# Fp16 queries from PSUM for the first two groups, short zero products in PSUM slots of their own, and a new issue order

## The chip, the cores and the metric

The kernel runs on one core of a Trainium2 chip. The metric is the device time of one execution in microseconds (us): the median of several runs. The engines of the core are named as the profile names them: PE (matrix products and transposes, with PEld for its weight loads), DVE, ACT and POOL (elementwise work), and SP, whose queue (SPq in the profile) issues all DMAs of this kernel. Each engine executes its own instructions in the order in which they stand in its queue. An instruction that waits for a semaphore holds up everything behind it on its engine.

## The reference

Two stages are chained. The first is an attention with chunk selection over q, k, v of shape (4, 8, 768, 64): batch, head, token, dimension. Keys are cut into 24 chunks of 32. For each chunk the smallest and the largest key per dimension give an upper bound on the score:

```python
ub = np.sum(np.maximum(q[..., None, :] * k_min, q[..., None, :] * k_max), axis=-1)
ub = np.where(causal, ub, -1000000000.0)
top_chunks = np.argsort(ub, axis=-1)[..., -6:]
scores = scale * np.matmul(q, k.transpose(0, 1, 3, 2))
scores = np.where(sel & (pos[:, None] >= pos[None, :]), scores, -1000000000.0)
attn = softmax(scores); attn_out = np.matmul(attn, v)
```

The second takes the attention output as x (4, 768, 512), and mixes tokens and channels:

```python
theta = x @ w_theta
y = einsum('ts,bsd->btd', w_tok_r, x * cos(theta)) + einsum('ts,bsd->btd', w_tok_i, x * sin(theta))
u = x + y
out = u + np.maximum(u @ w_ch, 0.0)
```

## The kernel before, in words

Heads are handled in groups of four: group (b, g) is heads 4g to 4g+3 of batch b, so there are eight groups. A group is prepared by these steps.

- `load_kc` (L276), `load_q` (L285) and `load_v` (L295) fetch keys, queries and values in fp32. One `q32` buffer holds a pair of heads; its two loads are one per head.
- `keys` builds the chunk maxima and minima on DVE (L315, L320, L324), transposes them (L339) into `bnd`, casts the keys to fp16 on POOL (L351) and transposes them on PE (L359); ACT or DVE evicts them to `kext` (L365). Rows 64 to 87 of `kext` are a constant one-hot pattern times -1000, loaded by DMA (L766), which is needed before any scores of that `kext` buffer.
- `queries` transposes the fp32 queries on PE into the PSUM tile `psq` (L394). ACT (L402) or DVE (L404) makes the positive and the negative part in fp32 for the bounds (`ubq`). The fp16 queries for the scores come in one of two ways. For groups in the set `QPE` (before: only (0, 0)), ACT or DVE casts them out of the same `psq` tile straight into `qext` (L410), and block 0, which the bounds do not need, is transposed too. For the others, POOL casts the queries untransposed into `qe` (L381), and a DMA transpose takes them from there to `qext` (L479).
- `choice` makes the bounds (`psub`, L432), adds the causal mask (L440), transposes (L446), finds the sixth largest bound (L454) and marks the chunks below it (L468). For `QPE` groups the marks go to a small tile, are transposed on PE (`pss`, L492) and evicted to rows 64 to 87 of `qext` by ACT or DVE (L497, one instruction per head). For the others they are written into `qe` and travel with the queries in the DMA transpose L479, of which a group has two, one for each pair of heads.

`attend` then works head by head: scores (`psc`, L533) in three PSUM tiles from a pool of two slots ("sc"); exp on ACT (L542); the causal triangle of the diagonal blocks on POOL (L553); the product with the values (`psav`, L564); the division on DVE (L575, L580). When the eight heads of a batch are there, x is transposed (PE L608 or DMA L597) and `phases` computes theta (`pst`, L628), sine and cosine on ACT (L636) and their products with x on DVE (L642). `mixer` does the token product (L670, L672), the channel product (L706) and the output. The token weights are cast on POOL (L731), transposed on PE (L743) and evicted (L747); they share the 'w32' and 'a16' buffers. All short-lived PSUM tiles come from a pool of three slots ("mi").

At the start, `FILL` zero products (L832) of 128x128 by 128x512 keep PE at work while it waits for data. They write one tile of the pool "sc" and read a zeroed tile of the tag "cs".

All of this is registered as tasks with `plan.add`. `Plan.emit` does not sort: the constant tuple `ORDER` lists the task numbers in the order of issue (a negative number sends an eviction that may run on either engine to DVE instead of ACT). The durations, due times and latencies given to `plan.add` have no effect on the program: they served the planner that wrote `ORDER`. Each engine's queue is its part of that list.

Of the kernel before, what the change touches and what calls it, by code (L numbers as in the profile page):

```python
# [9 lines left out]
FP32 = mybir.dt.float32  # L10
FP16 = mybir.dt.float16
ALU = mybir.AluOpType
AF = mybir.ActivationFunctionType
# [62 lines left out]
def kernel(  # L76
# [14 lines left out]
    P = 128  # L91
# [22 lines left out]
    for r in range(96):  # L114
# [40 lines left out]
        18, 0, 14, 17, 16, 2, 19, 8, 1, 7, 9, 54, 3, 20, 4, 21, 5, 22, 83, 55, 23, 6, 15, 84, 188, 117, 24, 72,  # L155
        25, 86, 87, 26, 27, 85, 58, 28, 73, 29, 88, 190, 30, 74, 62, 31, 60, -90, 32, 118, 76, 67, 64, 119, 75,
        65, 66, 63, 61, 56, 90, -72, 91, 77, 96, 69, 33, 93, 57, 34, 78, 35, 70, 36, 120, 37, -100, 68, 38, 189,
        39, 10, 79, 98, 40, 41, 80, 94, 42, 121, 43, -93, 44, 191, 11, 45, -98, 95, 81, 146, 82, 297, 100, 101,
        192, 150, 13, 102, 106, 59, 103, 46, 104, 194, 107, 296, 115, 47, 131, 48, 130, 108, 132, 49, 122, 50,
        133, 105, 154, 109, 137, 110, 298, 51, 111, 151, 52, 53, 138, -115, -114, 174, 124, 193, 147, 175, 180,  # L160
        299, 139, 116, 125, 112, 140, -149, 181, 126, 252, 134, 300, 123, 253, 258, 195, 196, -153, 182, 135,
        177, 127, 259, 141, 178, -150, 176, 266, 129, -154, 260, 136, 128, 142, 155, 310, 200, 254, 255, 156,
        311, 12, -158, 313, 329, 143, 179, -313, 183, 316, 314, 415, 158, 267, -316, 184, 144, 256, 280, 185,
        334, 159, 172, 145, 272, 186, 160, 257, 281, 301, 161, 268, 302, 335, 336, 187, 317, 283, 416, 273, 417,
        284, 269, 318, 304, 325, 261, 337, 197, 262, 418, 339, 286, 166, 162, 204, 270, 319, 167, 163, 419, 338,
        263, 201, 264, 164, 326, 327, 282, 265, 271, 165, 328, 168, 274, 287, 173, 169, 202, 170, 285, 330, 203,
        320, 198, 199, 288, -333, 429, 303, 275, -332, 276, 322, 431, 305, 448, 321, 294, 208, 277, -296, 308,
        -431, 444, 453, 323, -455, 306, 456, 278, 324, 279, 205, 458, 171, 353, -456, 309, 457, 359, 354, 289,
        307, 340, 351, 360, 626, 435, 212, 356, 420, 290, 367, 357, 355, 291, 423, 206, 341, 292, 368, 627, 373,
        209, 361, -208, 374, 370, 293, 345, 216, 436, 371, 381, 625, 342, 358, -383, 383, 343, 369, 389, 384,  # L170
        346, 372, 344, 390, 386, 375, 347, 362, 432, 364, 387, 385, 210, -435, 363, 391, 348, 397, 333, 365, 349,
        639, 398, 366, 213, -212, 376, 378, 641, -434, 377, 352, 403, 628, 379, 214, 404, 421, 400, 217, -216,
        640, 629, 401, 422, 218, 642, -220, 405, 388, 220, 445, 644, 380, 350, 449, 402, 643, 437, 392, 394, 399,
        450, 393, 472, 395, 658, 224, 396, 473, -447, 406, 408, 424, 428, 654, 407, -452, 447, 478, 475, 409,
        410, 474, 411, 476, 413, -413, 663, -415, 479, 666, 477, -665, 486, 667, -666, 470, 668, 582, 487, 490,
        221, 480, 452, 228, 222, 585, 743, 488, 425, 491, 494, 492, 489, 426, -224, 225, 481, 498, 495, 427, 496,
        493, 744, 226, 232, 502, -228, 229, 499, 630, 500, 483, 482, 497, 236, 506, 632, 501, 503, 510, 631, 504,
        484, 471, 485, 511, 507, 745, 230, 505, 508, 512, 634, 438, 583, 522, 523, 524, 509, 525, 233, 513, 514,
        586, 439, 240, 515, 588, 441, 635, 231, 516, 596, 237, 526, 440, 589, 527, 584, 244, 597, 587, 234, 528,
        633, 637, 599, 442, 590, 600, 602, 443, 238, -236, 746, 241, 591, 593, -240, 636, 610, 645, 517, 246,  # L180
        459, 518, 742, 603, 646, 242, 611, 604, 460, 592, 613, 594, 464, 680, 243, 461, 616, 462, 465, 614, 534,
        601, 747, 245, 535, 463, 617, 536, 247, 466, 248, 558, 598, 250, 559, 595, 537, 618, 647, 624, 605, 607,
        612, 538, 467, 539, 615, 540, 249, 606, 560, 546, 468, 608, 651, 609, 547, 251, 561, 748, 548, 648, 619,
        519, 469, 649, 562, 520, 946, 563, 650, 549, 638, 521, 682, 564, 683, 621, 762, 620, 685, 550, 686, 551,
        688, 681, 552, 652, 689, 696, 653, 751, 529, 763, 697, 702, 669, 947, 690, 622, 623, 749, 530, 687, 764,
        754, 703, 699, 684, 756, 670, 700, 750, 711, 698, 674, 759, -758, 671, 704, 712, -759, 714, 672, 662,
        691, 693, 692, 655, 760, 761, 673, 701, 949, 717, 715, 694, 531, -657, 768, 771, 695, 718, 675, 532, 705,
        657, 706, 713, 676, 725, 707, 719, 753, 533, 728, 726, 708, 677, 541, 716, 710, 659, 709, 553, 660, 731,
        -543, 720, 722, 678, 775, 727, 543, 554, -662, 732, 721, 765, 570, 729, 950, 776, 571, 739, 723, 544,
        730, 572, 573, -779, 733, 772, 752, 724, 574, 975, 948, -774, 575, 799, 576, 797, 734, 735, 736, 800,  # L190
        -778, 555, 755, 737, 951, 774, 738, 802, 679, 801, 556, 740, 803, 780, -742, 798, 783, 805, -785, 813,
        804, 806, 545, -786, 955, 1064, 903, 807, -782, 814, -783, 557, 766, 565, 953, 808, 817, -567, 1065, 767,
        815, 917, 818, 821, 816, 819, 825, 820, 822, 823, 966, 829, 826, 827, 567, 824, 833, 828, 830, 831, 568,
        809, 834, 569, 810, 577, 835, 769, -579, 954, 832, 904, 579, 770, 779, 952, 958, 786, 580, 1066, 967,
        918, 787, 906, 791, 788, 907, 837, 789, 792, 909, 790, 910, 931, 838, 793, 848, 911, 932, 839, 811, 968,
        908, 849, 840, 794, 920, 905, 919, 841, 812, 795, 921, 934, 972, 912, 836, 913, 935, 937, 850, 969, 796,
        842, 938, 851, 922, 843, 852, 957, 979, 914, 923, 915, 1067, 960, 916, 924, 976, 844, 853, 961, 925,
        1003, 978, 854, 1006, 1001, 926, 855, 1004, 870, 970, 871, 1007, 872, -963, 581, 927, -978, 1063, 984,
        928, 1009, 1008, 945, -986, 873, 1010, 929, 939, 874, 875, 1011, 956, 1017, 876, 933, 1068, 1020, 1018,
        930, 987, 936, 845, -990, -987, 1005, 1021, -989, 1019, 940, 942, 963, 846, 941, 983, 980, 943, -966,  # L200
        1023, 881, 1022, 1024, 971, 882, 964, 883, 944, 884, -983, 859, 1031, 1002, 885, 981, 1012, 1096, 847,
        860, 886, 887, 1069, 861, 1032, 1083, 1033, 862, 973, 863, 892, 974, 864, 865, 893, 1084, 1038, 866, 894,
        1039, 1035, 1085, 1013, 856, 1036, 1072, 1086, 895, 877, 896, 897, 959, 1014, 857, 867, 898, 1075, 858,
        1089, 888, 1015, 1025, 990, 868, 1092, 1016, 899, 878, 991, 1034, 1040, 995, 992, 879, 1046, 1026, 869,
        993, 1028, 1047, 1077, 1073, 1052, 996, 994, 1074, 1078, 1027, 1053, 1054, 1048, 997, 1049, 880, 889,
        1079, 1050, 998, 1080, 1037, 1029, 890, 999, 900, 1081, 1051, 1030, 1082, 1097, 901, 1093, 1098, 1000,
        1087, 1041, 1101, 1043, 1099, -1095, 1042, 1044, 1060, 1045, 1095, 1104, 1088, 1055, 1057, 1106, 1070,
        1120, 1103, -1106, 1090, 1102, 891, 1056, 1121, 1091, 1126, 902, 1058, 1107, 1059, 1127, 1128, 1061,
        1108, 1123, 1062, 1112, 1122, 1109, 1113, 1124, 1110, 1134, 1111, 1125, 1100, 1230, 1135, 1224, 1114,
        1129, 1130, 1138, 1115, 1136, 1117, 1142, 1139, 1137, 1146, 1140, 1143, 1071, 1141, 1150, 1144, 1147,  # L210
        1145, 1148, 1151, 1154, 1131, 1149, 1158, 1152, 1159, 1155, 1160, 1161, 1156, 1169, 1225, 1170, 1171,
        1132, 1157, 1153, 1172, 1076, 1162, 1173, 1231, 1116, 1163, 1174, 1175, 1227, 1164, 1226, 1202, 1228,
        1133, 1232, 1203, 1165, 1119, 1204, 1238, 1180, 1229, 1176, 1118, 1233, 1239, 1234, 1181, 1205, 1252,
        1191, 1253, 1235, 1192, 1244, 1236, 1254, 1237, 1245, 1241, 1240, 1206, 1242, 1246, 1207, 1243, 1267,
# [12 lines left out]
        1405, 1406, 1417, 1418,  # L227
    )
    PHK = -2
    FILL = 34  # L230

    UDMA = {(b, t) for b in (1, 2) for t in range(NT)} | {(3, t) for t in range(4)}
    XDMA = {(b, c) for b in (1, 2, 3) for c in range(3)}
# [655 lines left out]
```

## Time and profile before

| | us |
|---|---|
| median of 6 runs | 263.17 |
| lowest, highest | 262.22, 265.62 |
| the profiled execution, its own time | 263.93 |
| its span, first to last instruction | 262.2 |
| PE busy | 231.5 |
| DVE, ACT, POOL busy | 179.8, 159.7, 132.8 |

The profile page gives busy times by engine, then the span in 40 slices, the DMA queues, the chain of work that ended last, the costliest groups of instructions by line, and the DMA issues. A line of a group reads: line, engine, operation, output<-input, shapes, count, then busy time and the mean duration of one in ns, then the idle time of the engine just before and what ended it. A line of a timeline reads: start, duration, engine, line, operation, and in square brackets the idle time before it and its releaser. A line of the windows reads: stretch, length, busy time (and instructions) of PE, PEld, DVE, ACT and POOL, the granted PE clock, the busy share of the DMA engines and their GB/s.

### The profile page before, as it was taken

The numbers are of one execution on the slowest core, as the hardware profiler recorded it, in microseconds if no ns is written. First come the engines' busy times: TensorE is split into PE (matmuls) and PEld (weight loads), VectorE is DVE, ScalarE is ACT, GpSimd is POOL, SyncE is SP. The second block draws the span as 40 slices with busy tenths as digits, with TensorE's granted clock in tenths as the row PEclk, the third lists the DMA queues.
The fourth block names the chain that finished last, engine by engine and source line by source line (L and its number), as shares of the span: only waits on it lengthen the run. The fifth ranks groups of instructions, "written<-read, shape, count | busy, mean of one in ns | idle before, by whom it ended". The sixth has DMA issues, their size and how long they took to land.

```text
span 262.2 us, 5663 instructions
## 1 busy us (share of the span) xinstructions
PE 231.5 (88%) x2123; PEld 144.0 (55%) x2123; DVE 179.8 (69%) x470; ACT 159.7 (61%) x225; POOL 132.8 (51%) x188
## 2 busy tenths in 40 slices
PE   3877678688779999999989999997899999999993
PEld 1444365557655566577645666554654666644441
DVE  2779958758654988998997968669673335663362
ACT  2553858639659884299589765417698677654001
POOL 4366568776766658698920767263132554400000
PEclk9999569659979999999999999999999999999999
DMA  6998989999997999995974397477733206730234
GB/s 177 247 227 193 212 194 244 210 182 225 211 210 204 256 220 247 177 230 130 199 201 114 62 199 174 104 119 184 191 71 65 43 0 113 180 123 0 78 82 160
DMA packets 96674, 42.32 MB, mean 161 GB/s; under 512 B 89848, under 2 KB 90104, under 8 KB 95976
## 3 DMA queue, kind: packets, MB, share of 16 engines
q1 hardware_dynamic: 96648, 41.98, 72.9%
q8 instruction: 16, 0.26, 0.5%
q14 instruction: 10, 0.08, 0.1%
HBM read 26.30 MB, written 6.29 MB: 124 GB/s over the span
## 4 chain that ended last, share of the span: by engine, by line
PE 61%; DMA 15%; DVE 7%; ACT 7%; POOL 4%; SPq 4%; issue 2%; DVEq 0%; POOLq 0%; ACTq 0%
PE psc L533 11%; PE psy L670 8%; PE psy L672 8%; PE psav L564 6%; PE pst L628 6%; PE pso L706 5%; DMA qext<-qe 5%; PE psub L432 3%; SPq L295 3%; DMA out_dram<-ot 2%; DMA w<-in_moe_w_tok_i_dram 2%; PE psz L670 2%; PE psz L672 2%; DMA q<-in_q_dram 2%; PE psq L394 2%
## 5 line engine op out<-in xcount | busy, mean ns | idle before, releaser
L542 ACT ACTIVATE pt<-psc 128x1024 f16<-128x1024 f32 (+1 forms) x96 | 85.1, 920 | 45.7 <-PE psc L533 42.8
L553 POOL TENSOR_TENSOR pt<-pt,tri 128x256 f16<-128x256 f16 x96 | 65.4, 699 | 53.9 <-ACT pt L542 53.6
L533 PE MATMUL psc<-qext,kext 88*128 88x512 f16 (+3 forms) x256 | 55.6, 328 | 6.3 <-DMA qext<-qe 3.0
L533 PEld LDWEIGHTS <-kext 88*128 88x128 f16 x256 | 34.5, 154 | 22.2 <-issue 9.6
L670 PE MATMUL psy<-zz,wtokT 128*128 128x512 f16 x120 | 45.5, 379 | 0.0
L672 PE MATMUL psy<-zz,wtokT 128*128 128x512 f16 x120 | 45.4, 378 | 0.0
L564 PEld LDWEIGHTS <-pt 128*128 128x128 f16 x672 | 30.7, 101 | 8.1 <-POOL pt L553 0.9
L564 PE MATMUL psav<-v,pt 128*128 128x65 f16 x672 | 33.2, 198 | 1.0 <-DVE x L580 0.5
L402 ACT ACTIVATE ubq<-psq,signs 128x384 f32<-128x384 f32 (+1 forms) x38 | 18.2, 511 | 14.1 <-PE psq L394 14.0
L642 DVE TENSOR_TENSOR zz<-x,cs 128x1024 f16<-128x1024 f16 x24 | 17.4, 734 | 12.4 <-ACT cs L636 12.3
L706 PE MATMUL pso<-wch,uT 128*128 128x512 f16 x96 | 24.5, 379 | 1.3 <-ACT uT L698 0.5
L628 PE MATMUL pst<-wtheta,xT 128*128 128x512 f16 x96 | 23.3, 378 | 0.8 <-ACT cs L636 0.8
L315 DVE TENSOR_TENSOR h<-kc 96x1024 f32<-96x1024 f32 (+1 forms) x16 | 20.0, 1251 | 4.3 <-DMA kc<-in_k_dram 4.2
L394 PE MATMUL psq<-ident,q 128*128 128x128 f32 x82 | 17.0, 316 | 6.2 <-issue 2.1
L670 PEld LDWEIGHTS <-wtokT 128*128 128x128 f16 x144 | 14.1, 98 | 13.5 <-issue 0.7
L711 DVE SCALAR_TENSOR_TENSOR ot<-pso,u 128x512 f32<-128x512 f32 x24 | 16.5, 687 | 7.4 <-PE pso L706 4.9
L672 PEld LDWEIGHTS <-wtokT 128*128 128x128 f16 x144 | 14.0, 98 | 13.2 <-issue 0.2
L682 DVE TENSOR_TENSOR u<-psy,x 128x512 f16<-128x512 f32 x20 | 13.7, 689 | 10.9 <-PE psy L672 10.9
L636 ACT ACTIVATE cs<-pst,pi 128x512 f16<-128x512 f32 x24 | 16.7, 695 | 7.0 <-PE pst L628 6.1
L351 POOL CAST ke<-kc 96x1024 f16<-96x1024 f32 x16 | 17.2, 1079 | 3.7 <-DMA kc<-in_k_dram 2.7
L506 POOL CAST v<-v 128x768 f16<-128x768 f32 x16 | 15.0, 937 | 7.7 <-DMA v<-in_v_dram 4.4
L575 DVE RECIPROCAL rec<-psav 128x6 f32<-128x6 f32 x32 | 6.1, 191 | 18.4 <-PE psav L564 18.3
(72 smaller groups left out, 341.6 us busy)
## 6 DMA issues: line engine op xcount, KB each, us to landing
v<-in_v_dram SPq DMA_DIRECT2D x64, 96.0 KB, 3.9
q<-in_q_dram SPq DMA_DIRECT2D x32, 192.0 KB, 3.9
out_dram<-ot SPq DMA_DIRECT2D x24, 256.0 KB, 2.3
kc<-in_k_dram SPq DMA_DIRECT2D x7, 768.0 KB, 7.5
w<-in_moe_w_tok_r_dram SPq DMA_DIRECT2D x6, 384.0 KB, 4.3
w<-in_moe_w_tok_i_dram SPq DMA_DIRECT2D x6, 384.0 KB, 5.6
w<-in_moe_w_theta_dram SPq DMA_DIRECT2D x4, 256.0 KB, 6.4
w<-in_moe_w_ch_dram SPq DMA_DIRECT2D x4, 256.0 KB, 4.2
```

Source lines behind the costliest of these rows:

```text
L315: nc.vector.tensor_tensor(out=st[hn].rearrange("p (z w) d -> p z (w d)", z=2)[:, s], in0=kv[:, s, 0], in1=kv[:, s, 1], op=op)
L394: nc.tensor.transpose(t[:, o * P:(o + 1) * P], st[q32][:, n, :, :].rearrange("p x d -> p (x d)"), ident32)
L402: nc.scalar.activation(out=o, in_=i_, func=AF.Relu, bias=0.0, scale=signs[:, y:y + 1])
L533: nc.tensor.matmul(t[:, a0:a1], kx[0:KX, hj:CH * 96:NCH], qx[0:KX, q0 + a0 - o:q0 + a1 - o], start=True, stop=True)
L542: nc.scalar.activation(out=t[:, BASE[s]:BASE[s] + wa + wb], in_=st[psc][:, 0:wa + wb], func=AF.Exp, bias=0.0, scale=scale)
L553: nc.gpsimd.tensor_tensor(out=d, in0=d, in1=tri16.unsqueeze(1).broadcast_to([P, 2, P]), op=ALU.mult)
L564: nc.tensor.matmul(t[:, a, :], st[pt][:, o:o + P], v16s[g][:, x, j, :], start=(j == 0), stop=(j == a))
L628: nc.tensor.matmul(p, st[xT][:, c, t * P:(t + 1) * P], wtheta16[:, c, :], start=(c == 0), stop=(c == 3))
L642: nc.vector.tensor_tensor(out=st[zz][:, t, :, :].rearrange("p i (c d) -> p i c d", d=P), in1=st[cs].rearrange("p i (c d) -> p i c d", d=P) ...
L670: nc.tensor.matmul(acc(), wtokT16[:, i, 0, t * P:(t + 1) * P], st[zz][:, i, 0, :], start=(i == 0), stop=False)
L672: nc.tensor.matmul(acc(), wtokT16[:, i, 1, t * P:(t + 1) * P], st[zz][:, i, 1, :], start=False, stop=(i == NT - 1))
L706: nc.tensor.matmul(p, st[uT][:, c, :], wch16[:, c, :], start=(c == 0), stop=(c == 3))
```

## The change

Three things are edited. `QPE` now holds (0, 1) as well as (0, 0), so that the second group of batch 0 takes the way through PSUM. The zero products get a persistent zeroed tile `zero16`, `FILL` falls from 34 to 24, and six new tasks `rest` of two zero products each (together 36 products) write tiles of the pool "mi". `ORDER` is replaced as a whole; the assignment of evictions to ACT or DVE changes with it (241 tasks on ACT instead of 217, 295 on DVE instead of 307). One latency given to the planner changes, without effect on the instructions.

```diff
     ORDER = (
-        18, 0, 14, 17, 16, 2, 19, 8, 1, 7, 9, 54, 3, 20, 4, 21, 5, 22, 83, 55, 23, 6, 15, 84, 188, 117, 24, 72,
...
+        0, 1, 3, 8, 50, 2, 4, 5, 114, 6, 54, 52, 115, 113, 193, 7, 15, 17, 13, 14, 51, 18, 20, 21, 22, 47, 53,
...
-    FILL = 34
+    FILL, REST = 24, 6
...
-    QPE = {(0, 0)}
+    QPE = {(0, 0), (0, 1)}
...
-            dma(key, 786432 // parts, 280, go, w=[(n, z)], nw=[n] if z == 0 else [], lat=2.8)
+            dma(key, 786432 // parts, 280, go, w=[(n, z)], nw=[n] if z == 0 else [], lat=1.9 if parts == 2 else 2.8)
...
-    fz = ("cs", "zero")
-    plan.add("DVE", 0.45, -9.5, lambda: nc.vector.memset(new(fz), 0.0), w=[(fz, 0)], new=[(fz, "cs")])
-    plan.add("ACT", 1.5, -9.5, lambda: nc.scalar.activation(out=dmy, in_=st[fz][:, 0, 0:1], func=AF.Exp, bias=0.0,
-                                                            scale=1.0), r=[(fz, 0)], w=["table"], kind="exp")
+    zero16 = per.tile([P, dm], FP16, name="zero16", tag="zero16")
+    plan.add("DVE", 0.45, -9.5, lambda: nc.vector.memset(zero16, 0.0), w=["zero"])
+    plan.add("ACT", 1.5, -9.5, lambda: nc.scalar.activation(out=dmy, in_=zero16[:, 0:1], func=AF.Exp, bias=0.0,
+                                                            scale=1.0), r=["zero"], w=["table"], kind="exp")
     for i in range(FILL):
         def fill(i=i):
             t = newp(("fill",), "sc", [P, 1024], FP32) if i == 0 else st[("fill",)]
-            nc.tensor.matmul(t[:, 0:512], st[fz][:, 0, 0:P], st[fz][:, 0, :], start=True, stop=True)
-        plan.add("PE", 0.43 if i < 8 else 0.22, 0, fill, r=[(fz, 0), "ident32"], w=[(("fill",), 0)],
+            nc.tensor.matmul(t[:, 0:512], zero16[:, 0:P], zero16, start=True, stop=True)
+        plan.add("PE", 0.22, -9.4 + 0.2 * i, fill, r=["zero"], w=[(("fill",), 0)],
                  new=[(("fill",), "sc")] if i == 0 else [])
+    for i in range(REST):
+        def rest(i=i):
+            t = newp(("rest", i), "mi", [P, dm], FP32)
+            for _ in range(2):
+                nc.tensor.matmul(t, zero16[:, 0:P], zero16, start=True, stop=True)
+        plan.add("PE", 2 * dm * MM, -3 + i * 0.6, rest, r=["zero"], w=[(("rest", i), 0)], new=[(("rest", i), "mi")])
     prepare(0, 0)
```

What the new order does to the queues up to the first scores of batch 1, read from the lists of both programs. SP: before the second one-hot load (L766) stand 9.52 MB of loads instead of 8.73; up to and with the last query load of batch 1 10.41 MB instead of 11.00; up to and with the first DMA transpose of group (1, 0) 14.53 MB instead of 15.22, of which 0.79 MB are the two transposes that no longer exist. ACT: 31 instructions stand before the first exp instead of 19, among them the casts of all four query pairs of batch 0. PE: the scores of heads 4 to 7 of batch 0 begin right behind the transposes of the second group's marks; the transposes of the last query pair of batch 1 stand behind the first scores of head 4 instead of ahead of them. From the first theta product on, PE's list has the same work.

## The prediction

> **What bounds the kernel now.** I read the stretches first, each engine's busy time between marks that I chose at the first scores, at the two halves of batch 0, and where PE gets dense:
>
> ```profile
> 0.00:25.00 25.00, 16.70 (x119) 9.05 (x120) 16.64 (x47) 10.50 (x20) 13.33 (x28) 1.00 0.97 206
> 25.00:55.00 30.00, 22.21 (x205) 16.69 (x204) 22.91 (x60) 19.53 (x30) 19.73 (x28) 0.71 1.03 215
> 55.00:80.00 25.00, 20.66 (x257) 15.74 (x256) 16.34 (x54) 17.49 (x24) 18.02 (x25) 0.87 1.14 220
> 80.00:135.00 55.00, 52.93 (x548) 34.31 (x547) 47.44 (x122) 40.24 (x55) 40.06 (x52) 1.00 0.89 203
> 135.00:230.00 95.00, 91.23 (x864) 55.63 (x863) 62.53 (x172) 64.12 (x84) 41.69 (x59) 1.00 0.54 118
> ```
>
> From 80 us on PE is busy 96% at full clock: 182 us that only less PE work would shorten. Before 80 us PE has gaps, its clock sags to 0.71, and the one thing that is full is the DMA share, 0.97 to 1.14 at 206 to 220 GB/s. So the start is paced by transfers and what waits for them; a gain there moves the dense part forward whole. Next the chain that ended last, for that part:
>
> ```profile
> 28.77 4.16 SPq L295
> ...
> 48.15 4.88 DMA q<-in_q_dram
> ...
> 53.16 0.66 PE psq L394 x2
> ...
> 66.29 8.28 DMA qext<-qe
> ...
> 74.61 0.60 PE psc L533 x3
> ```
>
> It runs through SP's full queue, the last query load of batch 1 (landing at 53.03), its transposes, and the DMA transpose of group (1, 0), which lands 8.28 us after its issue and starts batch 1's scores at 74.61. The first theta product follows at 79.48. Last, the path that the change removes:
>
> ```profile
> 48.66 3.57 SPq L479 DMA_TRANSPOSE qext<-qe  x1
> ...
> 55.62 2.11 SPq L479 DMA_TRANSPOSE qext<-qe  x1
> ```
> ```profile
> 54.41 0.83 POOL L381 CAST qe<-q 128x768 f16<-128x768 f32 x1 [1.18 <-DMA qext<-qe]
> ```
>
> The marks of group (0, 1) are done on DVE at 47.8, its first transpose lands at about 54.4, and PE starts head 4's scores at 54.58; ACT is idle for 4.03 us before that.
>
> [...] six zero products from 7.03 take 2.56 us, 0.427 each; thirteen from 13.87 take 2.97, 0.228 each. But the granted clock reads 1.00 in both places, so that column is no proof in the first 10 us. [...] here L410 is on ACT and DVE alone. [...] here L479 lands after 3.7 to 8.3, median 4.3. [...]
>
> **The change part by part.** All durations are from the profiled execution (263.93 us, 1.73 more than its span, 0.76 above the median). I form a difference in its span and take it from the median.
>
> *Group (0, 1) through PSUM.* Gone: two POOL casts (L381, mean 868 ns: 1.74 us), two DMA transposes (5.68 us of SP issue, 0.79 MB). New: two fp32 transposes of block 0 (three take 0.49, so 0.33 us) and five fp16 ones (L492, 0.45) on PE; eight casts L410, seven on ACT (0.474) and one on DVE (0.559): 3.88 us; four evictions L497, three on ACT (0.681), one on DVE (0.49): 2.53. ACT gets 5.4 us, DVE 1.1, PE 0.8. In the first 25 us ACT is busy 10.50, and it idles 4.03 before 54.87: cover is there. Not all of it: the casts stand ahead of the first exp and the last ones wait for a load; I put the first exp (25.40) 1 to 2 us later. Without cover the ACT part would cost 5.4. After this delay the (0, 1) scores could start when marks (47.8), transposes and evictions are through: 47.8 less the 2 to 3 us by which its bounds stand nearer the front, plus 0.45 and 0.7, about 46 to 47; the second one-hot load, 0.79 MB later at 215 GB/s, is issued 3.7 us later than 38.26 and lands by about 46 as well. So head 4 starts near 47 instead of 54.58. That is 7.5 us for the half batch, but not for the end.
>
> *What is late next.* The last query load of batch 1 has 0.59 MB less ahead of it: 2.7 us, landing at 50.3. PE's queue has its transposes behind head 4, so PE may wait there for some 2 us at half work, which costs nothing against 54.58. The first transpose of group (1, 0) has 0.69 MB less ahead: 0.69 / 0.22 = 3.1 us, issue at 63.2, landing by the same 8.28 at 71.5 instead of 74.57. The second half's exps and triangles end earlier than that: POOL has 1.74 us less and begins them 5 to 7 us sooner, so the last value product stands behind batch 1's scores, as before. The bounds for the gain at this point are 0 (if q's landing doesn't move) and 5.5 (if the load queue empties and the landing takes the median 4.3). I take 3.1 and add 0.4 for a part of the shorter landing: 3.5.
>
> *Zero products.* 36 instead of 34, 0.216 warm: 0.4 us, while PE is busy only 16.70 of the first 25. I cost it at nothing; uncovered 0.4. The new "mi" tiles have no reader, so their slots are free at the product's end; a wait for a slot costs at most two products, 0.43. Their gain by the clock: the granted clock loses 30 x 0.29 + 25 x 0.13 = 12 us of half speed between 25 and 80; PE was waiting for most of it. I take zero, with bounds of a loss of 0.4 and a gain of 4 (a third).
>
> *The order after 80 us.* Same PE work, 14 further evictions moved from DVE to ACT beyond the ten above, the same eight table loads. Edits in the dense part can only add or remove waits: PE idles 2.1 us in 80 to 135 and 3.8 in 135 to 230, so at most 5.9 can be won, and ACT's load bounds the loss (below). I take zero. At the end, one output now stands ahead of the transpose of u's fourth block on SP; its product starts 0.4 us later than PE could. I charge 0.2 for that, as PE has other products to do there. Sum: -3.5 + 0.2 = -3.3, and 263.17 - 3.3 = **259.9**.
>
> **The rivals.** *The gain is eaten by the loads* (262.5): the stage is paced by bytes, and the transpose of (1, 0) stays tied to marks that come after the bounds of (1, 0), queued on PE behind more second-half scores than before. For it: PE's queue is strict and q lands only 2.7 us earlier. Against: 0.79 MB really leave. Gain 0.7. *The clock comes too* (255): psub took 2.0 us at 56.5 and 1.25 later; if the new order keeps PE warm from 25 to 80, 4 us of queued PE work go as well, 3.5 + 4 + some. Against: PE has idle time there anyway. *ACT becomes the limit* (267, slower): ACT gets 24 more instructions of about 0.6 us, 14 us, on 159.7. Exps stand behind them, only two score slots exist, and PE's strict queue stops when a slot is late. Today PE waits for exp 1.1 us in all. A third of the 14 us exposed costs 4.8; with 0.9 lost from the late first exp and none of the start gained, about 267. It decides from the point where these waits exceed the 3.5 us gained. Against: ACT is busy 40.24 of 55 in the densest stretch.
>
> **How the numbers follow.** Forecast 0.52, loads 0.23, clock 0.10, ACT 0.15. A measurement of this kernel tells about 1% (2.6 us) from no change: faster means below 260.5. The forecast lies there in about 0.8 of its cases (0.42), the clock case always (0.10), the loads case seldom (0.02): 0.54. Within 1%: 0.10 + 0.20 = 0.30. Slower: 0.15 and a remainder of the loads case, 0.16. The range runs from 254.5 (the clock case's centre, the bounds 5.5 plus part of 4) to 265.5 (loads case with a loss), leaving out most of the ACT case and the far side of the clock case. The forecast's own range is 257.7 (the gain of 5.5) to 262.5.
>
> **What would show it.** Right: L479 twelve times, L381 twelve; head 4's scores near 47; the transpose of (1, 0) issued near 63 and batch 1's scores near 71; the first theta product near 76; PE dense from there for the same 182 us. Wrong: head 4 early but batch 1's scores at 74 (loads); granted clock near 1 from 25 on and PE work shorter (clock); waits of L533 for L542 of several us after 80 (ACT). The forecast fails as well if the dense stretch, re-ordered throughout, has other waits than before.

## The result, and the profile after

The changed kernel took 261.81 us in the median of 28 executions (257.54 to 265.34), the kernel before, beside it, 263.93 (63 executions). The ratio of the changed kernel's time to that of the kernel before is 0.9914, 95% interval 0.9883 to 0.9945: 0.9% faster, 2.1 us by the medians, where 3.3 were forecast. Run again later, beside other kernels, it gave 259.74 against 261.60 us, ratio 0.9954 (0.9917 to 0.9991). Both kernels spread over some 8 us from one execution to the next; the ratios leave out executions more than 1.5% above the fastest of their kernel, the medians don't, and where the two disagree both are given.

The profiled execution took 264.52 us (span 262.6), more than the median, and so its time can't be set against before's 263.93. The same stretches as before, each engine's busy time between the marks:

```profile
0.00:25.00 25.00, 17.50 (x121) 8.99 (x122) 17.05 (x49) 14.34 (x30) 12.28 (x26) 1.00 1.01 208
25.00:55.00 30.00, 23.64 (x244) 17.54 (x245) 22.99 (x59) 25.22 (x38) 23.55 (x30) 0.77 1.01 216
55.00:80.00 25.00, 20.80 (x234) 16.48 (x232) 14.00 (x48) 16.38 (x24) 17.14 (x23) 0.73 1.04 217
80.00:135.00 55.00, 52.97 (x535) 33.78 (x534) 47.10 (x117) 42.87 (x60) 35.55 (x50) 1.00 0.95 202
135.00:230.00 95.00, 93.07 (x889) 57.74 (x888) 61.05 (x170) 68.39 (x92) 40.75 (x59) 1.00 0.53 115
```

The DMA share ahead of 80 us is as full as before. ACT has taken on work: 25.22 of the 30 us from 25 to 55, instead of 19.53. The granted clock from 55 to 80 fell from 0.87 to 0.73. Between 135 and 230 PE is busy 93.07 us instead of 91.23.

The chain that ended last, for the part that the forecast spoke of:

```profile
40.83 6.73 DMA kext<-onehot
...
47.61 1.93 PE psc L533 x6
...
62.42 9.60 DMA qext<-qe
72.02 0.04 issue
72.06 1.01 PE psc L533 x3
```

Head 4's scores start at 47.61 (forecast 47, before 54.58), released by the second one-hot load. The transpose of group (1, 0) is issued at 62.42 (forecast 63.2), and batch 1's scores start at 72.06 (forecast 71.5, before 74.61). So far the forecast holds. PE's timeline from there to the first theta product, with idle times in brackets:

```profile
62.24 0.50 PE L743 MATMUL pw<-ident,a 128*128 128x128 f16 x6
64.71 0.66 PE L394 MATMUL psq<-ident,q 128*128 128x128 f32 x2 [1.97 <-DVE x L580]
...
72.06 1.01 PE L533 MATMUL psc<-qext,kext 88*128 88x512 f16 x3 [0.92 <-DMA qext<-qe]
...
79.03 1.02 PE L628 MATMUL pst<-wtheta,xT 128*128 128x512 f16 x4
```

The first theta stands at 79.03, where 76 was forecast: 7 us after batch 1's scores instead of 4.9. In the kernel before it was:

```profile
79.48 1.02 PE L628 MATMUL pst<-wtheta,xT 128*128 128x512 f16 x4
```

So the scores came 2.55 us earlier and the first theta only 0.45. The three products at 72.06 take 1.01 us; at 25.36 three of them took 0.60. The clock explains most of it; the stretches of one microsecond around it, columns as above:

```profile
63.00:64.00 1.00, 0.00 (x0) 0.00 (x0) 1.00 (x3) 0.75 (x1) 1.00 (x3) 1.00 0.79 149
64.00:65.00 1.00, 0.29 (x2) 0.32 (x3) 0.72 (x1) 0.00 (x0) 1.00 (x2) 0.57 1.05 210
...
77.00:78.00 1.00, 1.00 (x8) 0.68 (x6) 0.58 (x2) 0.64 (x1) 0.21 (x1) 0.61 1.17 268
78.00:79.00 1.00, 1.00 (x19) 0.94 (x17) 0.58 (x2) 0.06 (x1) 0.86 (x2) 1.00 1.35 337
```

PE falls to half clock within the gap of 1.97 us in front of 64.71 and stays there for 13.7 us, from 64.1 to 77.8 (worked out from the means of 0.57 and 0.61). Two later profiles, shown below, tell what this cost between batch 1's scores and the first theta. The same list of instructions took 4.66 us at full clock (66.90 to 71.56), instead of 6.97. The list of the kernel before took 4.06 at full clock (71.13 to 75.19) and 4.87 in the first profile, where it too fell to half clock, from 75.1 to 78.5. So of the 2.1 us by which this stretch grew, 0.6 is work that the new order put into it and 1.5 is the clock.

### The profile page after: what moved, and what is told of

The parts are those of the page before. It is cut to its first block, busy times and chain, and to the rows that moved or that the text cites. A ratio compares the mean times of both kernels' runs of the same rounds, so it can differ in the third digit from the quotient of the medians.

```text
span 262.6 us, 5705 instructions
## 1 busy us (share of the span) xinstructions
PE 234.0 (89%) x2132; PEld 145.6 (55%) x2132; DVE 173.9 (66%) x458; ACT 173.0 (66%) x249; POOL 129.3 (49%) x186
## 4 chain that ended last, share of the span: by engine, by line
PE 62%; DMA 12%; ACT 12%; DVE 9%; issue 2%; POOL 1%; SPq 1%; ACTq 0%; DVEq 0%
PE psc L533 13%; PE psy L670 9%; PE psy L672 8%; PE psav L564 6%; PE pso L706 6%; PE pst L628 6%; DMA qext<-qe 4%; ACT pt L542 4%; PE psub L432 3%; DMA uT<-u 3%; ACT ubq L402 3%; DMA kext<-onehot 3%; PE psq L394 2%; ACT cs L636 2%; PE psz L670 2%; DVE h L315 2%
## 5 line engine op out<-in xcount | busy, mean ns | idle before, releaser
L542 ACT ACTIVATE pt<-psc 128x1024 f16<-128x1024 f32 (+1 forms) x96 | 85.0, 918 | 31.9 <-PE psc L533 27.7
L533 PE MATMUL psc<-qext,kext 88*128 88x512 f16 (+3 forms) x256 | 55.3, 336 | 8.7 <-DMA kext<-onehot 3.7
L533 PEld LDWEIGHTS <-kext 88*128 88x128 f16 x256 | 34.9, 153 | 23.9 <-issue 8.0
L706 PE MATMUL pso<-wch,uT 128*128 128x512 f16 x96 | 26.2, 400 | 3.7 <-DMA uT<-u 3.7
L402 ACT ACTIVATE ubq<-psq,signs 128x384 f32<-128x384 f32 (+1 forms) x45 | 21.5, 513 | 6.0 <-PE psq L394 5.9
L351 POOL CAST ke<-kc 96x1024 f16<-96x1024 f32 x16 | 18.9, 1187 | 8.1 <-PE pkt L359 3.9
L365 ACT COPY kext<-pkt 64x768 f16<-64x768 f16 x19 | 15.1, 792 | 11.1 <-PE pkt L359 10.9
L394 PE MATMUL psq<-ident,q 128*128 128x128 f32 x84 | 15.9, 305 | 5.0 <-DVE x L580 2.0
L575 DVE RECIPROCAL rec<-psav 128x6 f32<-128x6 f32 x32 | 6.1, 191 | 18.4 <-PE psav L564 18.3
```

Source lines behind the costliest of these rows:

```text
L394: nc.tensor.transpose(t[:, o * P:(o + 1) * P], st[q32][:, n, :, :].rearrange("p x d -> p (x d)"), ident32)
L402: nc.scalar.activation(out=o, in_=i_, func=AF.Relu, bias=0.0, scale=signs[:, y:y + 1])
L533: nc.tensor.matmul(t[:, a0:a1], kx[0:KX, hj:CH * 96:NCH], qx[0:KX, q0 + a0 - o:q0 + a1 - o], start=True, stop=True)
L542: nc.scalar.activation(out=t[:, BASE[s]:BASE[s] + wa + wb], in_=st[psc][:, 0:wa + wb], func=AF.Exp, bias=0.0, scale=scale)
L706: nc.tensor.matmul(p, st[uT][:, c, :], wch16[:, c, :], start=(c == 0), stop=(c == 3))
```

## The experiments

Twelve runs followed, among them the changed kernel and the kernel before once more. The letters name the theories in the expectation printed with each run. Each ratio is to the kernel before, run beside it; the changed kernel itself ran again beside the runs "up to 170 us", "the old zero products" and "the one-hot load earlier" only. Where the order was edited, the same tasks stand elsewhere in `ORDER`; the edits are shown by the tasks' outputs. In kernels whose `ORDER` is printed in longer form the line numbers stand 10 higher.

**The tail.** In this profile PE's products L706 wait 3.7 us for transposes of u, 2.3 of them at the end, where the forecast charged 0.2.

```diff
 SP: uT(3,0), [- out(2,5)] uT(3,1), [+ out(2,5)] uT(3,2), [+ uT(3,3)] out(3,0), [- uT(3,3)] out(3,1) ...
 PE: pso(3,2), [- pso(3,3)] psut(3,5), pso(3,4), pso(3,5), [+ pso(3,3)]
```

> The changed kernel with its last stretch re-ordered: on SP the transpose of u's fourth block goes ahead of the output of block 0 and the output (2, 5) behind the transpose of block 1; on PE the channel product of block 3 goes last, behind the transposes and products of blocks 4 and 5. Nothing else moves. Theory A (the tail gives back what the start won; the 0.2 us that the prediction charged there is the wrong term): the 3.7 us that L706 waits for the transposes fall below 1 us, the last products run at full clock (8 products in about 1.9 us instead of 3.56), and the time falls by about 3 us against the changed kernel, to a ratio of 0.980 to the kernel before. Theory B (as the prediction summed it, the tail is worth 0.2 us, because the end is set by the stores of the outputs): 0.5 us at most, ratio 0.990.

Ratio 0.9858 (0.9813 to 0.9903), median 260.93 against 262.65, which is 0.9934; the changed kernel's two were 0.9914 and 0.9920. No gain that both measures show. What PE waited for behind 230 us, in total, times and longest, changed kernel first, mended tail second:

```profile
PE pso L706 <- DMA uT<-u: 2.3, 1, 2.3
```
```profile
PE pso L716 <- DVE ot L721: 2.7, 1, 2.7
```

The wait for the transpose is gone, and one for an output tile took its place: there are two of these, and DVE waited 3.46 us for the store of an earlier one. The last eight products take 2.31 us instead of 3.56. Of the 3.7 us of waits for transposes of u, which A saw below 1, 1.4 are left, all ahead of 230; A's 1.9 us for the last products did not come. That the stores of the outputs set the end, as B said, fits the trace. Against the changed kernel's ratios, 0.9914 and later 0.9954, the ratio allows 1.5 to 2.5 us of A's 3; the medians allow none.

**The start alone.**

```diff
 ORDER = the new one up to the first theta product,
-        the new one to the end
+        then what is left in the order of the kernel before
```

> The changed kernel's tasks and its order up to the first theta product; everything that is left then follows in the order of the kernel before, with its choice of ACT or DVE for the evictions. Theory B (the prediction: the start is worth all of the gain, the order after 80 us nothing): the ratio to before is that of the changed kernel, 0.991, or the 0.987 forecast if the tail alone was mis-sized. Theory A (the start gives only the 0.5 to 1 us that the profiled execution shows at the first theta and first psy, the re-ordered dense part gives some 3 and the tail takes 3 back): ratio 0.995 to 0.998, and no wait of L706 for transposes of over 1 us at the end.

Ratio 1.0002 (0.9968 to 1.0036), though its first theta stood at 72.27. From there to the end it took 187.2 us; the two profiles of the kernel before took 182.7 and 182.4, those of the changed kernel 183.6 and 183.2. The early start is worth nothing with the old rest behind it. That is against B; A was nearest with its ratio, though its reason, the tail, found no support above.

**PSUM way alone.**

```diff
-    QPE = {(0, 0)}
+    QPE = {(0, 0), (0, 1)}
 ORDER = that of the kernel before; the new tasks are put in behind what they read
```

> The kernel before with the second group's queries through PSUM and nothing else of the change: its own zero products and its own order, into which the casts, the transposes of the marks and their evictions are put (the marks' transposes ahead of the last query transposes of batch 1), two token weight tasks standing some places earlier. Theory B (two transposes and 0.79 MB less are worth most of the gain in any order): SP issues the first transpose of group (1, 0) some 3 us earlier than 66.29, first theta near 77.5, ratio 0.993. Rival E (only with the new order does it pay: here the scores of head 4 still stand behind query transposes whose load lands at 53, and the transpose of (1, 0) waits for marks, not for SP): first theta within 0.7 us of 79.5, ratio 0.998 to 1.004.

Ratio 1.0043 (1.0014 to 1.0072), medians 263.24 against 262.65: no gain, as rival E had it. The first theta, at 77.62, stood where B had it (77.5), but no gain in time came with it, and the two profiles of the kernel before, at 79.48 and 75.19, differ by more. The first transpose of group (1, 0) came later than the 66.29 of the kernel before, not earlier. DVE's last marks of that group and SP's issue, in this kernel:

```profile
67.75 0.46 DVE L478 TENSOR_TENSOR qe<-psut,top 128x144 f16<-128x144 f32 x2
```
```profile
68.27 1.55 SPq L489 DMA_TRANSPOSE qext<-qe  x1
```

in the changed kernel, with the start of its bounds:

```profile
56.62 1.31 PE L432 MATMUL psub<-ubq,bnd 64*32 64x320 f32 x32
```
```profile
61.51 0.83 DVE L468 TENSOR_TENSOR qe<-psut,top 128x144 f16<-128x144 f32 x4
```
```profile
62.42 6.14 SPq L479 DMA_TRANSPOSE qext<-qe  x1
```

and in the kernel before:

```profile
56.43 2.07 PE L432 MATMUL psub<-ubq,bnd 64*32 64x320 f32 x32
```
```profile
65.77 0.46 DVE L468 TENSOR_TENSOR qe<-psut,top 128x144 f16<-128x144 f32 x2
```
```profile
66.29 1.69 SPq L479 DMA_TRANSPOSE qext<-qe  x1
```

SP issues 0.06 to 0.08 us after the end of the last marks in these three, and so it does in four more profiles: the changed kernel and the kernel before again, full clock, and the one-hot load earlier. So what releases the transpose is the marks, and not the bytes ahead of it. From the start of the bounds (L432) to the end of the marks the kernel before takes 9.8 us (56.43 to 66.23), and 9.2 when profiled again, this one 10.5, the changed kernel 5.7 (56.62 to 62.34), and 5.8 when profiled again; the nine other profiles with the new order up to there take 5.7 to 7.6. The clock is a small part of this: in the first profile of the kernel before, the bounds ran mostly at half clock (2.07 us against 1.31), but the 9.2 stand in a profile with almost the whole stretch at full clock. The bounds themselves start no earlier; the new order puts the transposes L446 and the DVE steps L440 to L468 right behind one another.

**Full clock.**

```diff
+    WARM = {("psc", 0, 4, 0): 16, ("psq", 2, 0, 0): 16, ("psc", 1, 0, 0): 10}
     st[name] = ps[tag].tile(shape, dt, name=name[0], tag=tag)
+    w = min(shape[1], dm) if name in WARM else 0
+    for _ in range(WARM.get(name, 0)):
+        nc.tensor.matmul(st[name][:, 0:w], zero16[:, 0:P], zero16[:, 0:w], start=True, stop=True)
```

> The changed kernel with 42 more zero products, put into tiles that the next instruction overwrites: 16 of 512 columns before the scores of head 4, 16 of 256 before the first transposes of batch 2's queries, 10 of 512 before the first scores of batch 1. They fill the gaps of 3.75, 1.97 and 0.92 us in front of these. Theory C (the gain of 2.5 us at batch 1's scores is lost again up to the first theta because PE runs at half clock there): the granted clock from 45 to 80 us rises from about 0.75 to 0.9, the first theta comes 2 to 3 us earlier, and the time falls by as much against the changed kernel, ratio 0.982. Rival D (PE waits there for transfers, exps and slots, and a faster PE waits longer): no change in time or up to 1 us more, ratio 0.991 to 0.995, though the clock rises.

Ratio 0.9784 (0.9738 to 0.9830), six executions of 255.43 to 258.42: faster than the kernel before, by the ratios also faster than the changed kernel, and a spread of 3 us. The mean granted clock over these executions is 0.980, of the kernel before 0.956. The stretch from 45 to 80 us, changed kernel first, then this one:

```profile
45.00:80.00 35.00, 28.19 (x284) 21.94 (x285) 20.43 (x58) 23.11 (x33) 23.11 (x31) 0.71 1.05 217
```
```profile
45.00:80.00 35.00, 30.53 (x354) 22.18 (x353) 27.06 (x63) 26.62 (x38) 25.02 (x34) 1.00 0.93 211
```

The clock is full throughout, and the first theta came 3 us earlier than in that profile (76.04), as theory C said. It is no earlier than in the executions in which the gaps stay short (71.6 to 75.6 in the profiles below): there the products cost something, 16 of them 1.91 us in a place where the mended tail's profile had a gap of 0.89. In the three profiles with such products, this one and the two combinations below, the clock stays full from 36 to 230 us, and in each of the eleven others it falls at least once between 44 and 80. Where the gain in time arises is not shown. In this profile the first theta is later than in the second profile of the changed kernel (74.47); it is the rest that is shorter, 180.5 us against 183.2, and it idles less behind 135 us than the first (6.7 us against 8.5).

**The changed kernel again**, unchanged.

> The changed kernel itself once more, beside the other three. Theory F (each execution's time is decided by whether PE keeps its full clock between 45 and 80 us, and that by the jitter of single transfers: in one profiled execution the first transposes of batch 2's queries came after a gap of 1.97 us and PE then ran at half clock for 14 us with the first theta at 79.0, in two others with the same instructions up to there the gap was 0.89 us, the clock stayed full and the first theta came at 71.6 and 72.3): the times spread over some 8 us again, a faster execution has the higher mean clock, and if this profile shows a time under 260 its first theta stands before 74, if over 262 after 76. Rival G (the start does not decide, the rest does): first theta within 2 us of 79 whatever the time is. Ratio to before 0.990 to 0.994 either way.

The 22 executions spread over 6.3 us. The profiled one took 259.65 us with the first theta at 74.47, half a microsecond outside the band that F gave. The correlation of time and mean clock over the 22 executions is -0.72, over the first 28 it was -0.82. F holds in the main: here the gap ahead of the query transposes was gone, and one of 2.36 us came in front of batch 1's scores, with half clock from 68.1 to 71.5. In the mended tail's profile, whose instructions are the same up to there, no gap of this stretch reached 1 us:

```profile
61.16 0.39 PE L404 MATMUL psq<-ident,q 128*128 128x128 f32 x2
62.44 0.54 PE L574 MATMUL psav<-v,pt 128*128 128x65 f16 x12 [0.89 <-DVE x L590]
...
66.90 0.59 PE L543 MATMUL psc<-qext,kext 88*128 88x512 f16 x3 [0.44 <-DMA qext<-qe]
...
71.56 1.02 PE L638 MATMUL pst<-wtheta,xT 128*128 128x512 f16 x4
```

Three products take 0.59 us there and the first theta stands at 71.56, 7.5 us ahead of the first profile of the same start.

**Up to 170 us, and the old tail.**

```diff
 ORDER = the new one up to the bounds of (3, 0)     | up to about 205 us,
+        then what is left in the order of the kernel before
```

> The changed kernel's order up to the bounds of group (3, 0), near 170 us, then what is left in the order of the kernel before. With the old order from the first theta product on the ratio was 1.000, with the new order throughout it is 0.991. Theory H (the gain of the new order lies in the dense part between 80 and 170 us, where 14 evictions go from DVE to ACT and PE's waits for slots fall): ratio 0.991. Rival I (it lies behind 170 us, where the outputs, the theta of the last two batches and the tail stand): ratio 0.998 to 1.001.

Ratio 0.9952 (0.9917 to 0.9987), but the medians give 261.42 against 261.60, 0.9993. By the first it is as fast as the changed kernel beside it (0.9954), which is H, by the second it is I; not settled. Its PE idles 3.8 us between 135 and 230, like the kernel before (3.8 and 2.9), which suggests that the waits saved there lie behind 170.

> The changed kernel's order up to about 205 us, and from there what is left in the order of the kernel before. Theory J (bookkeeping of PE's idle time: against the kernel before, the new order wins 2 to 5 us ahead of 80 us and 1.9 us between 135 and 230, and loses 2.2 to 3 us behind 230, where the four kernels with the new tail idle 6.5 to 7.4 us and those with the old one 4.4 to 5.8): idle time of PE behind 230 us below 6 us and the waits between 135 and 230 as short as in the changed kernel; ratio 0.986 where the changed kernel has 0.991 to 0.995. Rival K (the old tail fits only the old order ahead of it, and the stores of the last six outputs end the kernel either way, as they did in the mended tail): ratio within 0.002 of the changed kernel's.

Ratio 0.9899 (0.9833 to 0.9964) in six executions; the interval holds what J and what K expected, and the medians, 260.25 against 262.26 or 0.9923, are the changed kernel's. Idle time behind 230 fell to 5.7 us, below the 6 of J, but from 135 to 230 it rose to 3.7: what left one stretch turned up in the other, which speaks for K.

**The old zero products.**

```diff
-    FILL, REST = 24, 6
+    FILL, REST = 34, 0
```

> The changed kernel with the zero products of the kernel before: 34 of them, all into one tile of the score slots, none in the three-slot pool; the twelve that went there stand as ten of these in the same places, and the zeroed tile stays the persistent one. As predicted (the zero products are worth nothing): ratio the same as the changed kernel's, 0.991, first scores within 0.4 us. Rival (the new products keep PE warm or take a wait for a slot away at the start, up to 4 us): ratio 0.995 or more.

Ratio 0.9939 (0.9910 to 0.9968), median 258.25 against 261.60, where the changed kernel beside it has 0.9954 and 259.74: nothing is lost without the new ones. In its profile a late key load put the first scores at 27.73, 2.6 us behind the changed kernel's second profile (25.12), and the bounds of group (1, 1) at 93.39 against 93.11: the delay was gone by then.

**The one-hot load earlier.**

```diff
 SP: ... q(1,2) first half, [+ q(1,2) second half, one-hot 1] v(1,0) x4, [- q(1,2) second half] kc(1,1), [- one-hot 1] ...
```

> The changed kernel with two loads moved forward on SP: a query load of batch 1 (which PE waited 0.89 us for) and the second one-hot load, both ahead of four value loads and a key load of batch 1. The one-hot pattern lands some 5 us earlier and the wait of 3 to 3.75 us in front of the scores of head 4 goes. Theory C (the clock decides from 45 to 80 us): without that gap PE is warm when head 4 starts and stays so, the first theta comes at 70 to 75, the times spread less and the ratio is 0.980 to 0.986. Rival D (head 4 is not on the path, the marks of group (1, 0) are): head 4 at 44.5, but the first transpose of (1, 0) issued as before near 62, ratio 0.989 to 0.993.

Ratio 0.9895 (0.9858 to 0.9932), median 257.99 against 261.60. Head 4 starts at 44.25, but the transpose of (1, 0) is issued at 62.88, since the marks are no earlier: that is rival D's path. The time does not decide: the ratio is D's, the medians give 0.9862, at C's edge, and the first theta, at 72.89, lies in C's band. The clock from 45 to 55 was 0.56, because the gap only moved:

```profile
44.25 1.04 PE L543 MATMUL psc<-qext,kext 88*128 88x512 f16 x6 [0.89 <-ACT qext L507]
47.63 1.34 PE L574 MATMUL psav<-v,pt 128*128 128x65 f16 x21 [2.33 <-DVE kext L375]
```

**The kernel before again**, unchanged.

> The kernel before itself, one more look. The five profiles of kernels with the new start that came after the first one have the first theta at 71.6 to 75.0, the one profile of before at 79.5. Theory J expects before's first theta at 76 to 79 in an execution near its median, idle time of PE of 19 to 21 us ahead of 80 us and near 4 us between 135 and 230. Rival L (the start of the kernel before comes as early as the new one in an ordinary execution, and its one profile was a late one): first theta below 75.

A single execution of 259.4 us, faster than all eleven beside it. Its batch 1 scores and its first theta:

```profile
71.13 0.59 PE L533 MATMUL psc<-qext,kext 88*128 88x512 f16 x3 [0.48 <-DMA qext<-qe]
```
```profile
75.19 1.03 PE L628 MATMUL pst<-wtheta,xT 128*128 128x512 f16 x4
```

PE idles 19.3 us ahead of 80, as J said, but the first theta lies between J's 76 and L's 75, and the execution is not the ordinary one that both spoke of. It does not decide. It does show that the start of the kernel before can come as early as 0.7 us behind that of the changed kernel's second profile (74.47), which took about as long.

**Combinations.** The 42 zero products with the old tail, then also with the one-hot load early and fewer products.

```diff
-    WARM = {("psc", 0, 4, 0): 16, ("psq", 2, 0, 0): 16, ("psc", 1, 0, 0): 10}
+    WARM = {("psc", 0, 4, 0): 4, ("psq", 1, 3, 0): 8, ("psq", 2, 0, 0): 8, ("psc", 1, 0, 0): 4}
```

> The changed kernel with the 42 zero products that gave 0.978 and with the tail of the kernel before. If the two gains are separate (theory J): 0.970 to 0.973, times within 3 us of one another. If the tail is worth nothing (rival K): 0.978.

> As the run before, with the second one-hot load and a query load moved forward on SP as well, and fewer zero products for the shorter gaps: 4 of 512 columns before the scores of head 4, 8 of 256 before the last query transposes of batch 1 and before the first of batch 2, 4 of 512 before the scores of batch 1. If the zero products need only bridge what gap is left: 0.968 to 0.972, first theta near 71. If each gap that varies from one execution to the next needs its full cover to keep the clock: 0.978 to 0.985 and a spread of over 4 us.

Ratios 0.9834 (0.9768 to 0.9900) and 0.9775 (0.9679 to 0.9871), medians 258.46 and 258.00 against 262.26, with six executions each, from 256.1 to 265.4 and from 254.5 to 260.8. The gains don't add (K). The second has the spread that was told for gaps without full cover; its ratio lies just outside the band told for them (0.978 to 0.985), its medians, 0.9838, inside. In its profile the first theta is at 73.01, where 71 was told. Neither is better than the 42 products alone. The two executions above 264 us in the first have a mean clock of 0.961 and 0.952, the other four 0.980 to 0.987; what took the clock from them is not known, as neither was profiled.

## Why the prediction was right, and where its reasons were not

The sum was right (259.9 forecast, 261.81 measured, inside the range), and so was the direction. In part this is luck. The gain of 2.1 and 1.9 us lies between the 3.3 of the forecast and the 0.7 of the rival of the loads; 261.81 is within the 1% of 263.17 that the forecast held to be no change; and the 3.1 us at its core came by another path than the one it names.

Nor did a gain at batch 1's scores move "the dense part forward whole". In the two pairs of profiles the scores start 2.55 and 2.8 us earlier, the first theta 0.45 and 0.72, and the rest takes 0.9 and 0.8 us longer. Where PE waits is seen from its idle time per stretch (length less busy time). The kernel before and the changed kernel, both profiled again at nearly equal spans, columns as in the stretches above:

```profile
0.00:80.00 80.00, 60.69 (x604) 42.95 (x605) 57.87 (x160) 51.64 (x79) 55.95 (x83) 0.89 1.07 220
80.00:135.00 55.00, 52.81 (x542) 33.61 (x539) 50.76 (x123) 38.51 (x53) 35.31 (x47) 1.00 0.87 204
135.00:230.00 95.00, 92.15 (x874) 56.51 (x873) 62.64 (x173) 64.27 (x85) 41.38 (x58) 1.00 0.52 120
230.00:257.60 27.60, 23.10 (x113) 10.31 (x110) 11.24 (x17) 5.28 (x10) 0.00 (x0) 0.98 0.25 76
```
```profile
0.00:80.00 80.00, 64.49 (x636) 43.05 (x637) 56.73 (x159) 60.27 (x97) 56.08 (x82) 0.87 1.02 219
80.00:135.00 55.00, 53.35 (x533) 33.78 (x531) 49.05 (x120) 42.26 (x59) 33.58 (x46) 1.00 0.98 215
135.00:230.00 95.00, 93.01 (x873) 57.38 (x872) 59.53 (x168) 67.88 (x90) 39.80 (x58) 1.00 0.46 103
230.00:257.70 27.70, 21.09 (x95) 9.09 (x93) 9.03 (x14) 2.35 (x4) 0.00 (x0) 0.90 0.27 86
```

| idle PE, us | to 80 | 80 to 135 | 135 to 230 | behind 230 | all |
|---|---|---|---|---|---|
| before, two profiles | 20.4, 19.3 | 2.1, 2.2 | 3.8, 2.9 | 4.4, 4.5 | 30.7, 28.8 |
| changed, two profiles | 18.1, 15.5 | 2.0, 1.7 | 1.9, 2.0 | 6.6, 6.6 | 28.6, 25.8 |
| start alone | 18.4 | 0.6 | 4.5 | 5.7 | 29.2 |
| PSUM way alone | 20.4 | 1.3 | 5.6 | 4.5 | 31.7 |
| old tail | 18.3 | 1.7 | 3.7 | 5.7 | 29.4 |

By the means of two: -3.1 to 80 us, -0.3, -1.4, and +2.1 at the end, together -2.6. This is not the gain in time, though the medians of the times say -2.1 and -1.9. The two kernels' spans are all but equal in both pairs (262.2 and 262.6, 257.6 and 257.7), because PE, where it idled less, was busy 2.5 and 3.2 us longer, with a mean clock of 0.941 instead of 0.954 and 0.950 instead of 0.965. In these pairs the change turned waiting into slower work and some more of it. Where an execution near the median wins its 2 us is therefore not shown. The start is the likely place: in the eight profiles with the new start and no further zero products the first theta stands at 71.6 to 79.0, half of them below 74.5, in the two of the kernel before at 75.2 and 79.5; but two are few. Single profiles of one kernel also differ by up to 2.6 us in a stretch.

*Group (0, 1) through PSUM.* Right as told: the first exp starts at 26.52, 1.1 later (forecast 1 to 2), head 4 at 47.61 (47), and the one-hot load is what comes last: PE stood still 3.75 us in front of head 4 for it, and what stands behind head 4 in its list with it. (PE's 2132 and DVE's 458 instructions start in this profile in the order in which the program lists them.) It isn't for the end, as said: moving that load changed head 4, not the transpose of (1, 0).

*What is late next: the step that failed.* "The first transpose of group (1, 0) has 0.69 MB less ahead of it" gave 3.1 us, and 66.29 did become 62.42 (64.09 and 60.55 in the second pair). But with the bytes gone and the old order it became 68.27, and in the seven profiles read for it SP issues 0.06 to 0.08 us after the end of the marks. The 3.9 us come from the new order on PE and DVE, 5.7 us from bounds to marks instead of 9.8; that they are near the 3.1 of the bytes is luck. The rival of the loads named the tie to the marks, and was right about the tie; it was wrong that the marks would be no earlier. Nor did the landing fall, for which 0.4 us were added: 9.60 and 7.7 us instead of 8.28 and 7.0.

*Zero products.* Right: worth nothing, by the run that keeps the old 34, and the start has slack for 2.6 us at the first scores. But the kernel with further zero products from 45 to 80 us, where the change has none, has a ratio of 0.978, the change 0.991 and 0.995. "PE was waiting for most of it", the reason given for a clock gain of zero, was wrong for the stretch from 72 to 79, where the chain that ended last runs over PE at half clock. (The 12 us of the forecast are lost time; the clock was at half for 24 us.)

*The order after 80 us.* Near zero as a sum and wrong as a reading: in idle time 1.4 us were won between 135 and 230 and some 2 lost at the end, and from the first theta on the changed kernel takes 0.9 and 0.8 us longer. (The 96% that the forecast gives PE from 80 us on holds up to 230; over all 182 us it is 94%.) What PE waited for between 135 and 230, two lines of the kernel before, then the changed kernel's longest:

```profile
PE psq L394 <- ACT kext L365: 1.2, 1, 1.2
PE psut L446 <- DVE ot L711: 1.1, 1, 1.1
```
```profile
PE pso L706 <- DMA uT<-u: 1.4, 1, 1.4
```

The tail's 0.2 was mis-sized: the wait there is 2.3 us, since fewer products of the mixer are left to cover it, and in the one order tried against it a wait for the store of an output took its place. That the early start and the later order pay only together (1.000 for the start alone) was not foreseen; why the old rest loses the start's gain was seen only as 187.2 us behind the first theta, with idle time of 4.5 us between 135 and 230 and 5.7 behind, and stays open.

*ACT becomes the limit.* It did not: no wait of L533 for L542 shows in PE's waits of the changed kernel behind 80 us.

## What to carry to other kernels

When a transfer seems late because of the bytes in front of it, look at when its last input was ready: an issue a few hundredths of a microsecond after a DVE step (here 0.06 to 0.08 us, in seven profiles) points to that step. Take the parts of a change that moves the order one at a time and in place: here the new start and the way through PSUM, each alone, are worth nothing. And where one kernel's times spread, look at the clock of PE microsecond by microsecond behind each gap; cheap products in the gaps that jitter can open kept the clock full from 36 to 230 us in all three profiles that had them, and the two lowest ratios here, both 0.978, belong to kernels that have them.

## What the hardware showed that was not expected

How cheaply PE loses its clock, and that the length of a gap alone does not tell. Between 20 us and the tail the fourteen profiles have twenty gaps of 1.97 to 3.75 us at full clock, and all were followed by half clock; of ten gaps of 1.62 to 1.92 us five were and five were not. In the first profile of the changed kernel the clock fell within the gaps in front of 47.61 and 64.71, and at 26.6, 1.2 us after the end of the one in front of 25.36. Two of the ten, in the start alone and in the last combination:

```profile
79.89 0.82 PE L753 MATMUL pw<-ident,a 128*128 128x128 f16 x6 [1.62 <-POOL a L741]
```
```profile
47.51 0.84 PE L578 MATMUL psav<-v,pt 128*128 128x65 f16 x21 [1.83 <-DVE kext L379]
```

Behind the gap of 1.62 us six transposes took 0.82 us, where six at full clock take 0.50 (84.86 in the same profile). Behind the longer one, of 1.83 us, 21 value products took 0.84 us; in the first profile of the changed kernel the same number took 1.31 at half clock (69.83). What decided between the two is not shown.

The way back was not the same each time either. The first profile of the changed kernel, columns as above:

```profile
69.00:70.00 1.00, 0.31 (x6) 0.20 (x5) 0.97 (x3) 0.30 (x1) 0.97 (x2) 0.50 1.45 296
...
71.00:72.00 1.00, 0.14 (x3) 0.05 (x1) 0.82 (x3) 0.00 (x0) 1.00 (x2) 0.50 0.99 366
72.00:73.00 1.00, 0.94 (x5) 0.59 (x5) 0.27 (x1) 0.00 (x0) 0.44 (x2) 0.50 0.97 315
...
76.00:77.00 1.00, 1.00 (x16) 0.76 (x14) 0.17 (x1) 0.79 (x2) 1.00 (x2) 0.50 0.78 256
77.00:78.00 1.00, 1.00 (x8) 0.68 (x6) 0.58 (x2) 0.64 (x1) 0.21 (x1) 0.61 1.17 268
```

The half clock from 64.1 to 77.8 holds two more gaps, of 0.69 us in front of 69.83 and 0.92 in front of 72.06. From there on PE is busy, and the full clock is back 5.7 us later. In the second profile of the same kernel PE is busy from 68.33 on, and the full clock is back at 71.5, 3.2 us later. Beside the mended tail's profile, where the clock was full there, batch 1's scores, which the transpose releases in both, started 1.43 us later (68.33 against 66.90), and the first theta 2.91 us later (74.47 against 71.56).
